# An opening rebuilt around the first batch, with low halves of the weights on GpSimd

## The chip, the cores and the metric

The kernel runs on one core of a Trainium2 chip. A core has a matrix engine (TensorE, PE in the profile), a vector engine (VectorE, DVE), an activation engine (ScalarE, ACT), a general engine (GpSimd, POOL) and a queue engine (SyncE, SP) that issues most transfers. Each engine works through its own instructions in the order in which the program gives them, and waits on semaphores for what the others produce. The metric is the time of one execution in microseconds, taken as the median of several runs.

## What is computed

```python
def _attn_ref(q, k, v, phi):          # 8 batches, 8 heads, 576 rows, 64 wide; phi has 32 columns
    a = phi - np.max(phi, axis=2, keepdims=True)
    a = np.exp(a)
    a = a / (np.sum(a, axis=2, keepdims=True) + 1e-09)
    k_m = np.einsum('bhsm,bhsd->bhmd', a, k)
    v_m = np.einsum('bhsm,bhsd->bhmd', a, v)
    scores = (1.0 / np.sqrt(64)) * np.matmul(q, k_m.transpose(0, 1, 3, 2))
    scores = scores - np.max(scores, axis=-1, keepdims=True)
    attn = np.exp(scores)
    attn = attn / (np.sum(attn, axis=-1, keepdims=True) + 1e-09)
    return np.matmul(attn, v_m)

def _moe_ref(x, w_in, w_out):         # x: 4608 x 512, w_in: 512 x 2048, w_out: 2048 x 512
    h = x @ w_in
    g = h - np.tanh(h)
    return g @ w_out
```

The attention of all batches, laid out as 4608 rows, is the x of the second function. The weights come as 64-bit floats; everything else is 32-bit.

## The kernel before

The 4608 rows are cut into 18 **units** of 256 rows, the 2048 hidden columns into four **quarters** (fb 0 to 3). For each pair of unit and quarter there are a product H (`mm1`: attention weights times a per-batch matrix P, 24 matmuls, or 48 narrower ones where a unit spans two batches), an activation in two steps a and b (`g1`, `g2`: a vector operation each, between ScalarE squares), a third step c (`g3`: the low half of the result, a subtraction), and a product M (`mm2`: 24 matmuls with a quarter of w_out). Every operand is split into two 16-bit halves, so a product takes three matmuls.

Batches have 576 rows: batch 0 serves units 0, 1 and a quarter of 2; batch 1 serves the rest of 2, unit 3 and half of 4. For each batch the attention is made in steps: the maximum over phi's rows (X, XP), the exponential (Y, or XR and YT), pooling of K and V (V, `pool_half`, line 189), its normalisation (N), a turn of the result (U, UV), the scores in two halves of 288 rows (S), and the softmax of those halves. In START it is A and B for batches 0 to 2: line 255 a reduction, line 256 a subtraction, line 257 the exponential, lines 294 to 298 the sum, its reciprocal, the product and a transpose, all on VectorE but the exponential; BH and BL split the result into halves (lines 472, 478). P and PL (`att_p`, `att_pl`) multiply the batch's V matrix with a quarter of w_in.

The weights are loaded as 32 raw blocks of 512 KB (i0 to i15 of w_in, o0 to o15 of w_out). Step T (`conv`) turns two blocks into 32-bit floats with six VectorE instructions (lines 336, 340, 344) and their high halves with two on ScalarE (line 356). Step L (`low_dve`, line 371) makes the low halves with two more on VectorE; one pair of blocks has it done on TensorE (E and K).

The whole opening, up to the first pairs of unit 4, stands in a string START: each word is a step, and the order of the words is the order in which the instructions go into each engine's queue (`in_order` fixes it). `i1:kv3` is a load of block i1 into the buffer kv3. A buffer is reused, so a load waits until the last reader of the buffer is done, and all loads behind it on SP wait too. The first M of a pair of quarters starts an accumulation, the second ends it; for units 0 to 3 the sum over quarters 0 and 1 is written to DRAM and read back in the second half (issued from GpSimd and SP, lines 615 and 646), where a VectorE operation adds it (line 630).

After START a loop over 54 slots (unit 4 quarter 2 to unit 17) takes over, with the attention of batches 3 to 7 placed by PLAN tables relative to the slots; there the softmax's subtraction, product and low half (lines 266, 278, 490) and the third step c (line 570) are on GpSimd. In START no computation is on GpSimd.

PSUM holds two buffers for H ("h"), one for the attention ("pa") and two for M ("o0", "o1").

Of the kernel before, what the change touches and what calls it, by code (L numbers as in the profile page):

```python
# [8 lines left out]
F32 = mybir.dt.float32  # L9
# [9 lines left out]
P = 128  # L19
# [56 lines left out]
N_CHECK = N_F1 + 2 * B + DF // P + DM // P  # L76


class Attention:
# [5 lines left out]
    def load(self, b, d):  # L85
        self.load_phx(b, d)
        self.load_pha(b, d)
        self.load_kv(b, d)
        self.load_q(b, d)
# [5 lines left out]
    def load_pha(self, b, d):  # L95
        nc = self.tc.nc
        d["e"] = self.big.tile([P, 5, 256], F32, tag="e", name=f"e{b}", bufs=1)
        nc.sync.dma_start(d["e"][:, 0:4, :], self.ins["pha"][b])
        nc.sync.dma_start(d["e"][0:64, 4, :], self.ins["pht"][b])

    def load_kv(self, b, d):
        nc, big = self.tc.nc, self.big
        for g in range(4):
            t = big.tile([P, 2, 5, 129], F32, tag=f"kv{g}", name=f"kv{b}{g}", bufs=1)
            nc.sync.dma_start(t[:, :, 0:4, :], self.ins["kva"][b, g])
            nc.sync.dma_start(t[0:64, :, 4, :], self.ins["kvt"][b, g])
            for r in range(2):
                d["kv", g, r] = t[:, r]

    def load_q(self, b, d):  # L110
        nc, big = self.tc.nc, self.big
        for g in range(2):
            x = big.tile([P, 2, S], F32, tag="q", name=f"q{b}{g}")
            nc.sync.dma_start(x, self.ins["qt"][b, g])
            for h in range(2):
                for t in range(2):
                    d["q", 2 * g + h, t] = x[:, h, HS * t : HS * t + HS]

# [959 lines left out]
```

## Time and profile before

| what | value |
|---|---|
| time, median of 3 runs (lowest to highest) | 678.02 us (677.35 to 679.01) |
| span of the profiled execution, first to last instruction | 680.2 us |
| last instruction of START on TensorE (M of unit 3, quarter 3) ends, loop begins | 207.9 us into the span |
| first H, first M | 54.2 us, 68.6 us |
| TensorE busy from 204 us to 640 us | 433.1 of 436 us |

For the profiled execution the page gives the span alone, 680.2 us, and no time of its own; the span is 2.2 us above the median of the three runs. The profile is one page (shares of engines, the span in 40 slices of 17 us, the chain that ended last, the costliest groups of instructions), and further views answer questions: groups of instructions by line and form, the engines' busy time in a stretch, the instructions in order of time, the chain of waits in order of time. A row of a time-ordered view gives start, duration, engine, line, operation, output and inputs with their shapes; "x2" is two merged in one row, and the duration then covers both.

### The profile page before, as it was taken

To read this page: it belongs to the slowest core of one execution; us is meant where nothing else is said; L and a number is where in the kernel's file an instruction comes from. 1 tells how busy PE (TensorE), PEld (TensorE's weight loads), DVE (VectorE), ACT (ScalarE), POOL (GpSimd) and SP (SyncE) were. 2 spreads that over 40 slices of the span, in tenths; PEclk is the share of its full clock that TensorE was granted. 3 is DMA by queue.
4 is the path that set the end of the run, shared out by engine and by line. 5 is a ranking of instruction groups with operands and counts; after the bars stand their busy time and mean duration, and the time that the engine had idled before them with its cause. 6 is when DMAs were issued, how large, how long until landed. Compare 5 with 4: busy or idle time off the path is not lost.

```text
span 680.2 us, 15541 instructions
## 1 busy us (share of the span) xinstructions
PE 645.6 (95%) x6616; PEld 453.7 (67%) x6616; DVE 529.5 (78%) x823; ACT 373.5 (55%) x503; POOL 211.0 (31%) x150
## 2 busy tenths in 40 slices
PE   2588999999999999999999999999999999999995
PEld 2355465664656567777777777777777777887774
DVE  6689999999887677866698768876887586867672
ACT  3246667565544456554565555646555587666541
POOL 0000000000001324452344344534453555455521
PEclk9789999999999999999999999999999999999999
DMA  8956534731341241225331523152415323234101
GB/s 311 359 186 253 197 114 155 219 124 63 133 132 59 83 157 70 68 69 167 97 111 49 177 80 129 38 185 79 137 37 178 98 101 123 79 115 138 60 32 37
DMA packets 38653, 84.99 MB, mean 125 GB/s; under 512 B 4272, under 2 KB 14128, under 8 KB 38576
## 3 DMA queue, kind: packets, MB, share of 16 engines
q1 hardware_dynamic: 37152, 79.59, 35.6%
q0 software_dynamic: 1280, 4.20, 1.6%
q8 instruction: 54, 0.88, 0.5%
q14 instruction: 23, 0.19, 0.1%
q10 hardware_dynamic: 144, 0.13, 0.1%
HBM read 72.37 MB, written 11.53 MB: 123 GB/s over the span
## 4 chain that ended last, share of the span: by engine, by line
PE 70%; DVE 21%; DMA 3%; issue 2%; ACT 2%; SPq 1%; DVEq 0%; ACTq 0%
PE hs L533 18%; PE o L664 12%; PE x L671 12%; PE o L671 9%; PE o L622 9%; PE pkv L189 3%; DVE h L547 3%; DVE h L556 3%; PE h L533 2%; PE pp L500 2%; DVE wt L340 2%; DMA kv<-in_kva_dram 2%; DVE wt L344 2%; DVE f L583 2%; PE psc L237 1%
## 5 line engine op out<-in xcount | busy, mean ns | idle before, releaser
L570 POOL TENSOR_TENSOR g<-h,g 128x1024 f16<-128x1024 f32 x54 | 118.7, 2197 | 246.9 <-ACT g L561 139.9
L533 PEld LDWEIGHTS <-ph 128*128 128x128 f16 x2304 | 176.7, 98 | 21.5 <-issue 6.2
L533 PE MATMUL hs<-ah,ph 128*128 128x256 f16 (+3 forms) x1088 | 145.8, 248 | 0.0
L547 DVE SCALAR_TENSOR_TENSOR h<-hs,u 128x1024 f32<-128x1024 f32 x52 | 63.5, 1221 | 99.1 <-ACT u L539 99.1
L561 ACT ACTIVATE g<-h 128x1024 f16<-128x1024 f32 x72 | 76.1, 1057 | 97.2 <-DVE h L556 97.2
L533 PE MATMUL hs<-al,ph 128*128 128x256 f16 (+3 forms) x544 | 122.1, 247 | 0.0
L552 ACT ACTIVATE u<-u,beta 128x1024 f32<-128x1024 f32 x72 | 82.7, 1148 | 62.6 <-DVE h L547 62.4
L664 PE MATMUL o<-wout_hi,g 128*128 128x512 f16 x416 | 100.6, 379 | 1.6 <-DVE r L731 1.5
L622 PE MATMUL o<-wout_hi,g 128*128 128x512 f16 x320 | 98.6, 379 | 0.7 <-ACT g L561 0.7
L556 DVE SCALAR_TENSOR_TENSOR h<-u,h 128x1024 f32<-128x1024 f32 x72 | 87.7, 1218 | 5.7 <-ACT u L552 5.7
L671 PEld LDWEIGHTS <-f 128*128 128x128 f16 x832 | 81.4, 98 | 9.4
L622 PEld LDWEIGHTS <-g 128*128 128x128 f16 x480 | 45.9, 98 | 58.1 <-issue 3.6
L539 ACT ACTIVATE u<-hs 128x1024 f32<-128x1024 f32 x52 | 53.1, 1022 | 56.2 <-PE hs L533 56.0
L671 PE MATMUL x<-bt,f 128*128 128x256 f16 x624 | 76.6, 273 | 0.0
L671 PEld LDWEIGHTS <-g 128*128 128x128 f16 x624 | 60.9, 98 | 20.8
L664 PEld LDWEIGHTS <-g 128*128 128x128 f16 x416 | 38.6, 98 | 48.4 <-issue 13.4
L583 DVE TENSOR_TENSOR f<-g 128x512 f16<-128x512 f16 x104 | 58.2, 599 | 3.4 <-POOL g L570 3.4
L622 PE MATMUL o<-wout_lo,g 128*128 128x512 f16 x160 | 60.6, 379 | 0.0
L533 PE MATMUL h<-ah,ph 128*128 128x256 f16 (+2 forms) x448 | 55.5, 242 | 0.4 <-DVE h L547 0.4
L533 PE MATMUL h<-al,ph 128*128 128x256 f16 (+2 forms) x224 | 47.9, 242 | 0.0
L646 POOL DMA_DIRECT2D d<-ot x8 | 5.6, 695 | 132.5 <-ACT ot L640 132.5
L512 DVE SCALAR_TENSOR_TENSOR ph<-pp,ph 128x1024 f16<-128x1024 f32 x32 | 38.9, 1217 | 2.6 <-ACT ph L507 2.4
(144 smaller groups left out, 947.3 us busy)
## 6 DMA issues: line engine op xcount, KB each, us to landing
kv<-in_kva_dram SPq DMA_DIRECT2D x40, 258.0 KB, 3.4
raw<-in_w_in_dram SPq DMA_DIRECT2D x16, 512.0 KB, 6.5
raw<-in_w_out_dram SPq DMA_DIRECT2D x16, 512.0 KB, 4.9
chk<-in_w_in_dram SPq DMA_DIRECT2D x16, 512.0 KB, 5.6
chk<-in_w_out_dram SPq DMA_DIRECT2D x16, 512.0 KB, 3.3
out_dram<-r SPq DMA_DIRECT2D x25, 256.0 KB, 2.8
kv<-in_kva_dram SPq DMA_DIRECT2D x12, 516.0 KB, 7.8
q<-in_qt_dram SPq DMA_DIRECT2D x20, 288.0 KB, 3.4
```

The costliest lines, as they stand in the source:

```text
L512: nc.vector.scalar_tensor_tensor(pl, pa, S_P / (S_V * S_W), ph, op0=ALU.mult, op1=ALU.subtract)
L533: nc.tensor.matmul(hp[:, k, tu : tu + w], px[:, g, cs], d[ax][:, g, ta : ta + w], start=(n == 0), stop=(n == 5),)
L539: nc.scalar.activation(uu, hp, AF.Square, scale=1.0 / (S_A * S_P))
L547: nc.vector.scalar_tensor_tensor(h3, hp, C2 * S_G / (S_A * S_P), uu, op0=ALU.mult, op1=ALU.mult)
L552: nc.scalar.activation(uu, uu, AF.Square, bias=c["beta"])
L556: nc.vector.scalar_tensor_tensor(h3, uu, CC, h3, op0=ALU.add, op1=ALU.mult)
L561: nc.scalar.activation(gg[:, 0], h3, AF.Copy)
L570: nc.gpsimd.tensor_tensor(gg[:, 1], h3, gg[:, 0], op=ALU.subtract)
L583: nc.vector.tensor_tensor(o, x, y, op=op)
L622: nc.tensor.matmul(o, gx[:, k, P * tt : P * tt + P], wx[:, 4 * fb + k, :], start=(first and k == 0 and wx is wout_hi and gx is gh), stop=( ...
L664: nc.tensor.matmul(o[th], gg[:, 0, k, P * th : P * th + P], wout_hi[:, 4 * fb + k, :], start=(first and k == 0), stop=False)
L671: nc.tensor.matmul(dst, a(1 - n, kk), b(n, kk), start=(new and kk == 0 and n == 0), stop=(end and kk == 1 and n == 1))
```

## The change

The order of START is rewritten, and some steps change the engine.

- The loads of START begin with the first quarter of w_in and batch 0 alone. phi comes in one transfer per batch instead of two, K and V in two of 1.06 MB and one of 264 KB instead of eight, q in two. Blocks that share a buffer kv2 or kv3 are loaded in pairs, still a transfer each.
- The exponential of batches 0 to 2 is made the one way (X, XP, Y): the way with a turn on TensorE (XR, YT) is gone. `less_top` subtracts the maximum with one operation over four chunks and two over 64 partitions by 128.
- L is on GpSimd for 12 of the 16 pairs: ScalarE first scales the 32-bit block in place, GpSimd subtracts the high half. Lv (4 pairs) stays on VectorE. E, K on TensorE are gone.
- c is on GpSimd for 10 of START's 18 pairs (c), on VectorE for 8 (cv); the two on TensorE (d) are gone.
- The softmax of batches 0 to 2 uses the loop's steps AM, AE, AD, AT, AS: the subtraction, the product and the low half are on GpSimd, five of those 18 on VectorE (AMv, ADv, ASv).
- Units 0 to 3 all do quarters 0 and 1 before any does quarters 2 and 3, with M00, M10, M11, M01, then units 2 and 3; unit 1's first accumulation uses a buffer "h". The partial sums are written by ScalarE's queue (OP, `save_part`), read back by R and finished by O.
- In the loop the pooling of a batch (V) stands one slot later than before for batches 4 to 7, and `less_top` takes the place of the former two GpSimd operations.

```diff
 START = """
-i1:kv3 i0:kv1 FX0 T00 o2:pp5 i2:pp3 L00 o3:pp4 i3:gg KV0 o4:h3 XR0 T09 YT0 o5:uu L09 T01 V0 L01 FX1 Z02 N0 Q0
-U0 i5:h3 T10 Z00 i4:gg L10 UV0 Z06 KV1 XR1 S00 A001 S01 i6:gg Z07 YT1 E02 V1 B001 A012 Z03 N1 B012 U1 UV1
-i7:kv3 K02 BH001 P00 Q1 T03 o0:kv1 BH012 PL00 Z04 Z05 BL001 BL012 Z01 o1:gg L03 S10 H00 P01 T08 PL01 W1 i13:gg
-a00 H10 L08 S11 o7:kv0 i9:kv1 b00 H01 a10 P11 d00 o6:pp5 A102 a01 M00 i8:kv2 T11 b01 i15:kv3 H11 L11 PL11 c01
-b10 i14:pp5 Q2 FA2 M01 B102 d10 BH102 P10 i11:pp4 M10 a11 T07 BL102 b11 o8:kv3 L07 H21 PL10 FX2 H20 c11 T04
-i10:pp5 a20 M11 a21 L04 b20 T05 b21 L05 H31 H30 i12:pp5 c20 M20 c21 a30 W0 T06 o9:kv0 P12 b30 o10:gg L06 PL12
-M21 P02 T12 c30 PL02 o15:pp5 a31 M30 H02 X2 XP2 b31 H12 L12 Y2 o14:h3 c31 o11:gg T15 a02 P03 a12 KV2 M31 L15
-PL03 b02 T13 o13:gg H22 V2 N2 b12 H03 L13 c02 P13 c12 PL13 M02 a03 o12:pp4 U2 a22 T14 b03 H13 L14 c03 b22 a13
-c22 UV2 H23 M03 S20 M12 a23 A201 b13 c13 B201 BH201 P20 M13 PL20 b23 H32 BL201 H33 a32 S21 FQ3 FA3 A212 b32
-B212 W2 M22 c32 P21 PL21 H40 c23 BH212 a33 b33 M23 c33 X3 H41 a40 P23 PL23 BL212 b40 a41 M32 P22 b41 PL22 c41
-M33 c40 KR30
+i1:pp2 i0:gg i2:pp3 FX0 i3:us X0 XP0 Z00 T01 FA0 Y0 KA0 KB0 V00 i4:kv2 Q00 T00 V01 L00 Q01 i6:kv3 Z00 FA1 N0 U0 L01
+o5:pp4 Z00 T02 S00 L02 AM00 S01 UV0 AM01 P00 AE00 AE01 T03 AD00 o4:us o3:pp3 AD01 PL00 AT00 AT01 L03 AS00 o0:gg o2:pp5
+P01 T10 L10 PL01 FX1 KA1 KB1 Q11 H00 AS01 Z00 X1 o1:pp2 a00 XP1 W0 Y1 H10 T09 L09 V10 b00 a10 V11 Q10 H11 N1 o6:gg c00
+o9:pp5 U1 T08 UV1 o8:us L08 b10 H01 o7:pp4 S10 a11 S11 c10 i10:kv3 T11 L11 Q21 T12 M00 AM10 P11 o11:pp5 W1 b11 AM11
+PL11 Q20 M10 c11 AE10 L12 a01 ADv10 P10 M11 AT10 AS10 i8:kv2 OP1 PL10 AE11 b01 o10:qt FA2 c01 H21 T05 L05 ADv11 AT11
+H20 AS11 i14:kv3 M01 FX2 a21 a20 OP0 T04 b20 b21 Lv04 H30 H31 c20 i12:kv2 P02 T13 c21 PL02 L13 a31 a30 M20 X2 KA2 KB2
+P12 b30 PL12 H02 T06 b31 H12 o12:kv2 XP2 M21 c30 Y2 V20 V21 OP2 M30 cv31 Lv06 a02 N2 T07 FA3 Lv07 P03 PL03 M31 OP3 b02
+H03 c02 a12 a03 T14 b12 cv12 U2 UV2 H13 L14 a13 b03 o14:kv3 T15 H22 M02 S20 M12 b13 cv03 P13 Lv15 AM20 a22 M03 PL13 P20
+cv13 W2 R0 O0 H23 R1 PL20 AE20 S21 FQ3 a23 M13 b22 cv22 b23 M22 P21 AMv21 O1 cv23 R2 AD20 PL21 AT20 X3 H33 AE21 H32 a33
+ASv20 M23 a32 b32 b33 O2 ADv21 H40 H41 cv33 c32 P22 a40 a41 PL22 M32 P23 M33 b40 b41 c40 PL23 AT21 R3 AS21 cv41 KR30 O3
 """
+W_TAG = ["pr" if p in (1, 3, 9, 11) else "ot" for p in range(16)]
...
+        d["e"] = self.big.tile([P, 9, 128], F32, tag="e", name=f"e{b}", bufs=1)
+        self.tc.nc.sync.dma_start(d["e"], self.ins["pha"][b])
...
+    def load_kv(self, b, d, rows=(0, 1)):
+        for r in rows:
+            t = self.big.tile([P, 4, 4, 129], F32, tag=f"kv{r}", name=f"kv{b}{r}", bufs=1)
+            self.tc.nc.sync.dma_start(t, self.ins["kva"][b, r])
+            for h in range(4):
+                d["kv", h, r] = t[:, h]
+            if r == 0:
+                self.load_kt(b, d)
+
+    def load_kt(self, b, d):
+        t = self.big.tile([P, 4, 129], F32, tag="kt", name=f"kt{b}", bufs=1)
+        self.tc.nc.sync.dma_start(t, self.ins["kvt"][b])
+        d["kt"] = t
+
...
+        x = self.big.tile([P, 4, HS], F32, tag=tag, name=f"q{b}{t}", bufs=2 if tag == "q" else 1)
+        self.tc.nc.sync.dma_start(x, self.ins["qt"][b, t])
...
+    def less_top(self, eng, e, m):
+
+        eng.tensor_tensor(
+            e[:, 0:8].rearrange("p (c r) x -> p c (r x)", r=2), e[:, 0:8].rearrange("p (c r) x -> p c (r x)", r=2),
+            m.unsqueeze(1).to_broadcast((P, 4, 256)), op=ALU.subtract,
+        )
+        for r in range(2):
+            rs = slice(64 * r, 64 * r + 64)
+            eng.tensor_tensor(e[rs, 8], e[rs, 8], m[rs, 128 * r : 128 * r + 128], op=ALU.subtract)
+
...
+    def pool_half(self, b, d, r, pa=None, ps=None):
+            pa = self.psum(f"pkv{b}{r}", ps)
+        rs = slice(64 * r, 64 * r + 64)
+                hs = slice(32 * h, 32 * h + 32)
+                x, y = (e[:, 2 * c + r, hs], d["kv", h, r][:, c]) if c < 4 else (e[rs, 8, hs], d["kt"][rs, h])
+                nc.tensor.matmul(pa[hs, r, 0:129], x, y, start=(c == 0), stop=(c == 4))
...
-        nc.gpsimd.tensor_tensor(s3, s3, m.unsqueeze(2).to_broadcast((P, NB, 32)), op=ALU.subtract)
+        (eng or nc.gpsimd).tensor_tensor(s3, s3, m.unsqueeze(2).to_broadcast((P, NB, 32)), op=ALU.subtract)
...
-        nc.gpsimd.tensor_tensor(s3, s3, z.unsqueeze(2).to_broadcast((P, NB, 32)), op=ALU.mult)
+        (eng or nc.gpsimd).tensor_tensor(s3, s3, z.unsqueeze(2).to_broadcast((P, NB, 32)), op=ALU.mult)
...
-        ts = [big.tile([P, 512], U32, tag="ot", name=f"wt{p}{i}") for i in range(2)]
+        ts = [big.tile([P, 512], U32, tag=W_TAG[p], name=f"wt{p}{i}") for i in range(2)]
...
-    def low_pe(p):
-        pw = low_ps.pop(p)
+    def low_pool(p):
+        lo = low_of(p)
         for i in range(2):
-            nc.tensor.matmul(pw[:, i], c["nid16"], his[p][:, i], start=False, stop=True)
-        nc.scalar.activation(low_of(p), pw, AF.Copy)
+            nc.scalar.activation(tfs[p][i], tfs[p][i], AF.Copy, scale=S_W)
+            nc.gpsimd.tensor_tensor(lo[:, i], tfs[p][i], his[p][:, i], op=ALU.subtract)
 
...
+        if first and u == 1:
+            t = ps_h.tile([P, 2, DM], F32, tag="h", name=f"o1h{fb}")
+            acc[u] = [t[:, i] for i in range(2)]
+        elif first:
             acc[u] = [ps_o.tile([P, DM], F32, tag=f"o{i}", name=f"o{u}{fb}{i}") for i in range(2)]
...
+    def load_part(u):
+        acc["r", u] = [big.tile([P, DM], F32, tag="pr", name=f"pr{u}{i}") for i in range(2)]
+        for r, p in zip(acc["r", u], parts[u]):
+            nc.sync.dma_start(r, p)
+    def save_part(u):
+        sc = 1.0 / (S_G * S_W)
+        parts[u] = []
+        for tt in range(2):
+            ot = big.tile([P, DM], F32, tag="pr", name=f"ot{u}{tt}")
+            nc.scalar.activation(ot, acc[u][tt], AF.Copy, scale=sc)
+            parts[u].append(dram.tile([P, DM], F32, tag=f"d{u}{tt}", name=f"d{u}{tt}"))
+            nc.scalar.dma_start(parts[u][tt], ot)
+    def save(u):
+        sc = 1.0 / (S_G * S_W)
+        for tt in range(2):
+            o, t0 = acc[u][tt], u * UT + P * tt
+            if u in parts:
+                ot = acc["r", u][tt]
+                nc.vector.scalar_tensor_tensor(ot, o, sc, ot, op0=ALU.mult, op1=ALU.add)
+            else:
+                ot = big.tile([P, DM], F32, tag="pr", name=f"ot{u}{tt}")
+                nc.scalar.activation(ot, o, AF.Copy, scale=sc)
+            nc.sync.dma_start(out[t0 : t0 + P, :], ot)
 
...
-        (-11, "FQ{0} FA{0}"), (-10, "; X{0} KR{0}0"), (-9, "| XP{0} YM{0}"), (-8, "; YE{0} | V{0}0 KR{0}1 N{0}0"), (-7, "| V{0}1 N{0}1 QT{0}0"),
+        (-11, "FQ{0} FA{0}"), (-10, "; X{0} KR{0}0"), (-9, "| XP{0} YM{0}"), (-8, "; YE{0}"), (-7, "V{0}0 KR{0}1 N{0}0 | V{0}1 N{0}1 QT{0}0"),
```

Functions that the new START doesn't call (`conv_p`, `to_size`, `att_pl_p`, `g1_p`, `g2_p`) are added as well and left out here.

More of the change, by code (lines that the diff above doesn't have):

```diff
@@ L88, in load @@
         self.load_kv(b, d)
-        self.load_q(b, d)
+        for t in range(2):
+            self.load_q(b, d, t, "q")
     def load_phx(self, b, d, tag="sc"):
@@ L609, in mm2 @@
         gh, gl = gg[:, 0], gg[:, 1]
-        if first:
+        if first and u == 1:
+            t = ps_h.tile([P, 2, DM], F32, tag="h", name=f"o1h{fb}")
+            acc[u] = [t[:, i] for i in range(2)]
+        elif first:
             acc[u] = [ps_o.tile([P, DM], F32, tag=f"o{i}", name=f"o{u}{fb}{i}") for i in range(2)]
-            if u in parts:
-                acc["r"] = [big.tile([P, DM], F32, tag="pr", name=f"pr{u}{i}") for i in range(2)]
-                for r, p in zip(acc["r"], parts[u]):
-                    nc.sync.dma_start(r, p)
-        both, low = ((wout_hi, gh), (wout_lo, gh)), ((wout_hi, gl),)
-        order = [(0, both), (0, low), (1, both), (1, low)] if last else [(0, both), (1, both), (0, low), (1, low)]
+        both, less = ((wout_hi, gh), (wout_lo, gh)), ((wout_hi, gl),)
+        order = [(0, both), (0, less), (1, both), (1, less)] if last else [(0, both), (1, both), (0, less), (1, less)]
         for tt, part in order:
@@ L1040, in tile_kernel @@
             wide_path(inner, tc, c, ins, out)
[L1043 removed]
+_INS = ["qt", "kva", "kvt", "pha", "phx", "w_in", "w_out"]
 def kernel(**inputs):
```

284 lines of the change are left out of this document (112 added, 172 removed).

## The prediction

> **What bounds the kernel now.** I read the page first, then the engines' busy time by stretch, then the chain of waits in order of time, then single instructions in order of time, and last the groups by line.
>
> ```profile
> span 680.2 us, 15541 instructions
> ```
>
> ```profile
> 0.00:17.00 17.00, 4.26 (x20) 3.78 (x20) 11.14 (x22) 6.04 (x8) 0.95 (x10) 1.00 0.90 311
> 17.00:34.00 17.00, 10.12 (x116) 5.11 (x116) 11.26 (x23) 4.05 (x10) 0.00 (x0) 0.76 1.05 359
> 34.00:51.00 17.00, 15.12 (x167) 8.71 (x168) 14.67 (x31) 7.25 (x13) 0.00 (x0) 0.84 0.57 186
> ...
> 204.00:640.00 436.00, 433.06 (x4672) 322.81 (x4671) 325.73 (x509) 252.22 (x343) 192.68 (x122) 1.00 0.33 105
> ```
>
> ```profile
> 68.58:207.89 139.31, 138.47 (x1234) 80.07 (x1233) 130.49 (x173) 83.36 (x105) 8.79 (x14) 1.00 0.41 139
> ```
>
> The columns are the stretch, its length, busy time (and count) of PE, PEld, DVE, ACT, POOL, the granted clock, the DMA share and GB/s. From 204 to 640 us TensorE is busy 433 of 436 us: the loop is bound by TensorE, and nothing in it gets faster unless TensorE gets less work. What can move is START. The loop's first instruction, and START's first H and M:
>
> ```profile
> 54.16 0.28 PE L533 MATMUL h<-ah,ph 128*128 128x256 f16 x1
> ...
> 68.58 0.38 PE L622 MATMUL o<-wout_hi,g 128*128 128x512 f16 x1
> ...
> 207.89 0.22 PE L533 MATMUL h<-ah,ph 128*128 128x128 f16 x1
> ```
>
> So START ends at 207.9. From the first M at 68.6 TensorE is busy 138.5 of 139.3 us: dense already, beside a VectorE that is busy 130.5. The time before the first M is therefore what can be shortened, and the work behind it. Before the first M there are few products; TensorE waits for VectorE (conversions and softmax), and VectorE at first for data:
>
> ```profile
> 12.20 9.07 DMA kv<-in_kva_dram
> 21.27 0.04 issue
> 21.31 4.99 PE pkv L189 x74
> ...
> 167.22 0.77 PE pp L500 x24
> 167.99 5.35 PE o L622 x24
> 173.35 5.24 PE h L533 x48
> ```
>
> The last K and V of batch 0 land at 21.3. The lower rows give the products' prices: M 5.3, P 0.75, H 2.62 (the row holds two).
>
> **TensorE's work behind the first M.** By the old word order: 16 M = 84.8, 15 H = 39.3, 9 P = 6.8, and V2, U2, XP2, S20, S21 and d10 together some 7.6 (estimates from their rows' neighbours): 138.5, against 139.3 measured, so the count holds. By the new order all of H00, H10, H11 and H01 stand ahead of the first M: 14 H remain, d10 (2.2) is gone, and one P more is left (10). That is -2.6 - 2.2 + 0.75 = -4.1: **135.2 us from the first M to the end of START**, if TensorE stays dense.
>
> **When the first M starts.** Its last input is the w_out half L08, behind T08 on VectorE. First the data. Ahead of the second half of batch 0's K and V now lie i1, i0, i2, i3 (2.10 MB), phi twice (1.18), K and V (2.38): 5.66 MB. The first slice moves 17 us x 311 GB/s = 5.29 MB, the rest at 359: 18.0 us, and with 2.7 us for half the pooling (4.99 us for 74 of 80 matmuls, halved and rounded up) N0 can start at **20.7**. Then VectorE's queue, in word order:
>
> ```profile
> 150.47 0.77 DVE L336 TENSOR_SCALAR wt<-raw 128x512 uint32<-128x512 uint32 x2
> 151.14 1.30 DVE L340 SCALAR_TENSOR_TENSOR wt<-raw,wt 128x512 uint32<-128x512 uint32 x2
> 152.34 1.30 DVE L344 SCALAR_TENSOR_TENSOR wt<-raw,wt 128x512 uint32<-128x512 uint32 x2
> 153.54 1.23 DVE L556 SCALAR_TENSOR_TENSOR h<-u,h 128x1024 f32<-128x1024 f32 x1
> 154.68 1.30 DVE L371 SCALAR_TENSOR_TENSOR wout_lo<-wt,wout_hi 128x512 f16<-128x512 f32 x2
> 155.90 1.23 DVE L566 TENSOR_TENSOR g<-h,g 128x1024 f16<-128x1024 f32 x1
> ```
>
> From start to start T costs 3.07, b 1.14, L on VectorE 1.22; a, PL and cv have the size of b. AT costs 0.78, S (as many elements) 0.84, AM 0.75, AD (a reduction and two operations on 18 numbers) 1.2:
>
> ```profile
> L298 DVE STREAM_TRANSPOSE af<-sc 128x576 f32<-128x576 f32 x4 | 3.1, 778 | 0.2
> ...
> L255 DVE TENSOR_REDUCE sm<-sc 128x18 f32<-128x576 f32 x4 | 2.9, 736 | 0.1
> ```
>
> From N0 to T08 stand five T (15.35), two S, two AM, two AD, two AT (7.1), two PL, a00, b00, a10 (5.7), X1, Y1 (3.3, by their elements), N0, N1 and UV0 (1.9, small operations, estimated): 33.4 us. Without any hindrance T08 ends at 54.1. But GpSimd now works beside it: five L, c00, and AM, AD, AS twice:
>
> ```profile
> L385 POOL TENSOR_TENSOR fy<-chk 128x512 f32<-128x512 f32 x32 | 33.6, 1065 | 0.0
> L490 POOL TENSOR_TENSOR al<-af,ah 128x576 f16<-128x576 f32 x10 | 13.0, 1305 | 8.0 <-ACT ah L489 7.8
> ...
> L266 POOL TENSOR_TENSOR sc<-sc,sm 128x576 f32<-128x576 f32 x10 | 11.6, 1160 | 0.0
> ```
>
> An L is two operations of the first row's size (2.13), c is 2.13 (219.10 below), the softmax steps 1.16 to 1.31: 10.7 + 2.1 + 7.4 = 20.2 us in this stretch. How much of it VectorE pays is the unknown of this case. Four rows of the loop show that it pays at times:
>
> ```profile
> 219.10 2.13 POOL L570 TENSOR_TENSOR g<-h,g 128x1024 f16<-128x1024 f32 x1 [7.94 <-ACT g L561]
> 226.49 3.09 POOL L570 TENSOR_TENSOR g<-h,g 128x1024 f16<-128x1024 f32 x1 [5.26 <-ACT g L561]
> ```
>
> ```profile
> 226.37 1.22 DVE L595 TENSOR_TENSOR bt<-wout_lo,bt 128x2048 f16<-128x2048 f16 x1
> ```
>
> ```profile
> L583 DVE TENSOR_TENSOR f<-g 128x512 f16<-128x512 f16 x104 | 58.2, 599 | 3.4 <-POOL g L570 3.4
> L512 DVE SCALAR_TENSOR_TENSOR ph<-pp,ph 128x1024 f16<-128x1024 f32 x21 | 25.5, 1215 | 0.5 <-ACT ph L507 0.3
> L583 DVE TENSOR_TENSOR f<-g,f 128x512 f16<-128x512 f16 x52 | 23.1, 444 | 1.8
> L583 DVE TENSOR_TENSOR f<-f,g 128x512 f16<-128x512 f16 x52 | 21.6, 415 | 0.0
> ```
>
> The GpSimd operation that met a VectorE operation with two inputs in SBUF took 0.96 us longer than alone, nearly what was left of that operation. The other way round, L583 takes 599 ns on average where its sister forms, of the same size, take 0.42 to 0.44: 104 x 0.17 = 18 us of waiting beside 193 us of GpSimd, a share of 0.1. In START about half of the time belongs to operations of that kind (16 T, 18 b, 8 cv, 4 Lv: 84 of 163 us of VectorE's work), in the loop a third (b and the forms of L583, some 170 of 472). So I take a **share of 0.2** of GpSimd's time as VectorE's wait; the ends are 0 (every meeting falls on operations with one SBUF input, as a, PL and the reductions) and 1. With 0.2 T08 ends at 33.4 + 20.7 + 4.0 = 58.1. L08 adds ScalarE's last high half and first scaling (some 0.6 each, half of L561's elements below) and two GpSimd operations (2.13), 3.5 us with hand-overs: **first M at 61.6**, 7.0 earlier than before.
>
> The Trainium skill, in "SBUF — State Buffer", section "Who interferes with whom", says that a VectorE instruction with two SBUF inputs and a GpSimd instruction that reads SBUF exclude each other for a whole instruction. The row at 226.49 agrees; that it holds for the conversions' operations (L340, L344) no row here shows, since they never met GpSimd. By that rule the share would lie nearer the half than 0.2, and the change would lose; it is the first rival.
>
> **Can the middle stay dense?**
>
> ```profile
> L561 ACT ACTIVATE g<-h 128x1024 f16<-128x1024 f32 x72 | 76.1, 1057 | 97.2 <-DVE h L556 97.2
> ```
>
> The tight place is M20, which needs b20 and c20. VectorE from T08 to b20: four T (12.3), ten a, b, PL (11.4), two ADv with their product (3.9), two AM, S, AT and a UV (5.0): 32.6 us; GpSimd beside it 19.8 us, a fifth is 4.0. So b20 ends at 94.7, c20 at 97.9 (1.06 for the high half, 2.13). TensorE gets there at 61.6 + four M, three P, four H (34.0) = 95.6: 2.3 late. H21 needs AS10: VectorE reaches AT10 at 78.7, and with 2.0 for ah and al 80.7, against 79.0 on TensorE, which the same lateness covers. Behind M21 VectorE has less to do than TensorE (some 71 against 82 us). For uneven hand-overs between four full queues I add 2 us (estimate; 0 at best, and the old order lost 0.8 in 139). ScalarE takes on 12 x 1.2 us of scaling, the four OP and their eight DMA issues, 125 us of work in 200: it has room, but its queue is in order, and OP1 waits there for M11 with AE11 and b01's high half behind it; at 79 to 82 us neither is due earlier.
>
> **Other edits.** Partial sums leave GpSimd's queue for ScalarE's: eight issues, hidden as above; without cover some 0.5 each, as a load on SP (estimate). The clock of the first slices (0.76, 0.84) can fall again with fewer warming matmuls (4 words Z for 8); H00 to H01 have 20 us for 10.5 us of work, so half the clock would still be covered. FX1 is queued on SP behind AT01 (its buffer), with K, V, q and o1 behind it. o1 is the last block that T08 needs, at 16.2 MB: at 359 GB/s it lands at 47.4, and T08 starts at 55: 7.6 us of cover. The loop's V one slot later, its larger transfers and the split GpSimd operation lie beside a TensorE that is busy 99%; I take 0, ends -2 and +3 (its idle time, and a slot's wait in one of four batches).
>
> **The sum.** START ends at 61.6 + 135.2 + 2.3 + 2.0 = 201.1, against 207.9: 6.8 us less. The span becomes 673.4; the medians shown are 2.2 below the span, so 678.0 - 6.8 = **671.2 us**, 1.0% faster.
>
> **Rivals.**
> 1. *GpSimd and VectorE exclude each other fully in START.* For it: 226.49; T is six operations of the kind in a row. Against it: the loop's share of 0.1. With s for the share the end of START is 191.1 + 40 s + 2: it decides from s = 0.37. At 0.5: 213.1, 5.2 us later, **683 us**, slower; at 1 it would be 233, 703 us.
> 2. *Nothing is won ahead of the first M, because the loads set T08.* The third slice moved only 186 GB/s. If the transfers behind FX1 ran at that rate, 11.4 MB by 34 us and 4.8 MB more would be 60 us, T08 5 later: 676 us. Then the larger transfers don't do what they are for. Near no change. ScalarE's or the hand-overs' losing the same 5 us gives the same.
> 3. *VectorE is really freed.* Share near 0 and no lateness: first M at 57.6, end 193, **663 us**. For it: by the prices above VectorE's work in START falls from 185 to 163 us (15 L become 4, -13; 16 c become 8, -9).
>
> **How the numbers follow.** About 0.3% (2 us) is what a measurement of this kernel can tell from no change. Forecast (665 to 676) 0.50; rival 3 and better 0.11; rival 2 and others that end within 0.3% 0.12; rival 1 0.22; worse than 690 by share or by stalls in the loop 0.05. Faster 0.61, same 0.12, slower 0.27. For 8 in 10 the range takes half of rival 3 and the milder half of rival 1: 660 to 685. The likeliest sign's own range is 660 to 676.
>
> **What would show it.** The first H near 41 (54.2 before); the first M near 62; the loop's first H near 201; T, b and Lv rows of START near their old means plus a fifth of GpSimd's busy time (60 us there). Long T rows, with L340 or L344 means well over 0.7 us, show rival 1; a VectorE wait for o0 or o1 shows rival 2; TensorE less than 95% busy after the first M shows my density wrong. The loop's span should stay 472 us; if it doesn't, the PLAN edit was mispriced.

## The result, and the profile after

| | before | after |
|---|---|---|
| time, median (lowest to highest) | 678.50 us (677.35 to 679.01) | 687.84 us (687.42 to 688.35) |
| first H, first M, loop's first H | 54.2, 68.6, 207.9 us | 42.3, 68.1, 214.2 us |

The change makes the kernel **1.4% slower**: ratio 1.0138, 95% interval 1.012 to 1.0156, 9.3 us. The forecast was 671.2 us, with a range of 660 to 685.

The page's first line after, and its engine line:

```profile
span 686.3 us, 15313 instructions
...
PE 636.2 (93%) x6546; PEld 445.1 (65%) x6546; DVE 523.9 (76%) x794; ACT 379.0 (55%) x513; POOL 278.2 (41%) x186
```

The busy time by stretch (length; PE, PEld, DVE, ACT, POOL; granted clock, DMA share, GB/s), and the three landmarks in order of time:

```profile
0.00:17.00 17.00, 3.00 (x10) 1.21 (x14) 8.02 (x16) 3.68 (x4) 0.99 (x11) 1.00 0.90 344
17.00:34.00 17.00, 11.23 (x152) 5.42 (x153) 12.82 (x25) 8.22 (x15) 9.41 (x8) 0.95 0.93 371
34.00:51.00 17.00, 8.99 (x60) 4.75 (x60) 16.83 (x22) 8.38 (x13) 9.86 (x8) 0.65 0.57 223
214.00:640.00 426.00, 423.26 (x4610) 316.58 (x4609) 320.00 (x502) 244.17 (x330) 191.04 (x123) 1.00 0.33 107
68.08:214.16 146.08, 138.16 (x1233) 78.16 (x1227) 126.03 (x159) 85.64 (x111) 47.88 (x27) 0.98 0.39 131
```

```profile
42.32 0.39 PE L527 MATMUL h<-ah,ph 128*128 128x256 f16 x1
...
68.08 0.61 PE L615 MATMUL o<-wout_hi,g 128*128 128x512 f16 x1
...
214.16 0.22 PE L527 MATMUL h<-ah,ph 128*128 128x128 f16 x1
```

Three things are to be seen. The loads are better: 344 and 371 GB/s in the first two slices (311 and 359 before; 325 and 360 in a second profile of the kernel before), and the first H comes 12 us earlier. The first M, which was to come 7 us earlier, comes 0.5 us earlier, and VectorE is busy 16.83 of 17 us ahead of it. Behind it TensorE is idle 7.9 of 146.1 us (0.8 of 139.3 before), at a clock of 0.98. The loop takes 686.3 - 214.2 = 472.1 us, as before (472.3; 470.9 in the second profile): nearly all of the loss lies in START.

What fills VectorE shows in its rows in order of time, and in GpSimd's of the same moments:

```profile
58.32 3.07 DVE L338 TENSOR_SCALAR wt<-raw 128x512 uint32<-128x512 uint32 x2
...
82.18 1.70 DVE L271 TENSOR_SCALAR sz<-sz 128x18 f32<-128x18 f32 x1
...
91.35 3.22 DVE L346 SCALAR_TENSOR_TENSOR wt<-raws,wt 128x512 uint32<-128x512 uint32 x2
...
105.14 1.28 DVE L396 SCALAR_TENSOR_TENSOR win_lo<-wt,win_hi 128x512 f16<-128x512 f32 x2
106.34 0.76 DVE L338 TENSOR_SCALAR wt<-raw 128x512 uint32<-128x512 uint32 x2
107.02 1.28 DVE L342 SCALAR_TENSOR_TENSOR wt<-raw,wt 128x512 uint32<-128x512 uint32 x2
108.22 1.28 DVE L346 SCALAR_TENSOR_TENSOR wt<-raw,wt 128x512 uint32<-128x512 uint32 x2
109.43 1.22 DVE L499 SCALAR_TENSOR_TENSOR ph<-pp,ph 128x1024 f16<-128x1024 f32 x1
111.53 1.23 DVE L541 SCALAR_TENSOR_TENSOR h<-h,u 128x1024 f32<-128x1024 f32 x1 [0.89 <-POOL g L572]
```

```profile
56.55 2.28 POOL L404 TENSOR_TENSOR wout_lo<-wt,wout_hi 128x512 f16<-128x512 f32 x2 [6.10 <-ACT wt L403]
58.79 2.31 POOL L572 TENSOR_TENSOR g<-h,g 128x1024 f16<-128x1024 f32 x1
...
81.72 2.13 POOL L572 TENSOR_TENSOR g<-h,g 128x1024 f16<-128x1024 f32 x1
...
91.36 2.67 POOL L572 TENSOR_TENSOR g<-h,g 128x1024 f16<-128x1024 f32 x1 [2.89 <-issue]
...
105.30 8.28 POOL L572 TENSOR_TENSOR g<-h,g 128x1024 f16<-128x1024 f32 x2 [5.38 <-PE h L527]
```

An operation on 18 numbers a partition (L271 at 82.18) takes 1.70 us and ends at 83.88, just behind a GpSimd subtraction that began at 81.72 and ends at 83.85. T08's first step waits in the same way for L09 and c00 (3.07 us, to 61.39; GpSimd is done at 61.10). The other way round, the third step c of two pairs, c20 and c21, takes 8.28 us in place of 4.26: c20 begins at 105.30, while VectorE goes from one such operation to the next until 109.43; there L499 begins, which has one input in PSUM, and 2.1 us later c20 is done and lets L541 go. TensorE waits for that c (1.12 us ahead of the rest of M20, at 111.56).

TensorE's longest single wait behind the first M is not for GpSimd's result but for the exponential of batch 2, ahead of V20:

```profile
128.15 1.95 PE L189 MATMUL pkv<-kv,e 128*32 128x129 f32 x32 [2.96 <-ACT e L173]
```

It too begins with a meeting. VectorE's first step of T06 takes 2.69 us in place of 0.75, beside c30 on GpSimd (118.92 to 121.15):

```profile
118.75 2.69 DVE L338 TENSOR_SCALAR wt<-raws 128x512 uint32<-128x512 uint32 x2
```

The steps behind it come as much later, among them b31 and the subtraction that the exponential needs (L154 and L160, done at 126.6); the exponential starts at 126.94. Of the 7.9 us of idle time 3.0 are this wait, 3.6 waits for c and al, and 0.8 one for a low half that VectorE makes.

### The profile page after: what moved, and what is told of

It reads as the page before. It is cut to its first block, busy times and chain, and to the rows that moved or that the text cites. A ratio compares the mean times of both kernels' runs of the same rounds, so it can differ in the third digit from the quotient of the medians.

```text
span 686.3 us, 15313 instructions
## 1 busy us (share of the span) xinstructions
PE 636.2 (93%) x6546; PEld 445.1 (65%) x6546; DVE 523.9 (76%) x794; ACT 379.0 (55%) x513; POOL 278.2 (41%) x186
## 4 chain that ended last, share of the span: by engine, by line
PE 69%; DVE 8%; ACT 2%; issue 1%; DMA 1%; POOL 0%; ACTq 0%; SPq 0%; DVEq 0%
PE hs L527 18%; PE o L662 12%; PE x L669 12%; PE o L669 9%; PE o L615 8%; PE h L527 3%; PE pkv L189 3%; PE pp L487 2%; DVE f L585 2%; DVE h L557 2%; DVE h L541 1%; PE psc L232 1%; ACT u L533 1%; DMA kv<-in_kva_dram 1%; PE o1h L615 1%
## 5 line engine op out<-in xcount | busy, mean ns | idle before, releaser
L572 POOL TENSOR_TENSOR g<-h,g 128x1024 f16<-128x1024 f32 x64 | 144.9, 2265 | 304.4 <-ACT g L567 189.6
L541 DVE SCALAR_TENSOR_TENSOR h<-hs,u 128x1024 f32<-128x1024 f32 x52 | 63.5, 1222 | 97.0 <-ACT u L533 97.0
L553 ACT ACTIVATE u<-u,beta 128x1024 f32<-128x1024 f32 x72 | 82.7, 1148 | 61.6 <-DVE h L541 61.6
L662 PE MATMUL o<-wout_hi,g 128*128 128x512 f16 x416 | 100.6, 380 | 1.6 <-DVE r L729 1.6
L557 DVE SCALAR_TENSOR_TENSOR h<-u,h 128x1024 f32<-128x1024 f32 x72 | 89.0, 1239 | 4.5 <-ACT u L553 4.5
L615 PE MATMUL o<-wout_hi,g 128*128 128x512 f16 x256 | 79.3, 381 | 1.1 <-POOL g L572 1.1
L615 PE MATMUL o<-wout_lo,g 128*128 128x512 f16 x128 | 49.0, 383 | 0.8 <-DVE wout_lo L396 0.8
L499 DVE SCALAR_TENSOR_TENSOR ph<-pp,ph 128x1024 f16<-128x1024 f32 x32 | 38.9, 1214 | 3.7 <-ACT ph L494 3.4
L494 ACT ACTIVATE ph<-pp 128x1024 f16<-128x1024 f32 x32 | 32.6, 1017 | 11.8 <-PE pp L487 11.8
```

The lines of the kernel that those rows point to most:

```text
L499: nc.vector.scalar_tensor_tensor(pl, pa, S_P / (S_V * S_W), ph, op0=ALU.mult, op1=ALU.subtract)
L541: nc.vector.scalar_tensor_tensor(h3, hp, C2 * S_G / (S_A * S_P), uu, op0=ALU.mult, op1=ALU.mult)
L553: nc.scalar.activation(uu, uu, AF.Square, bias=c["beta"])
L557: nc.vector.scalar_tensor_tensor(h3, uu, CC, h3, op0=ALU.add, op1=ALU.mult)
L572: eng.tensor_tensor(gg[:, 1], h3, gg[:, 0], op=ALU.subtract)
L615: nc.tensor.matmul(o, gx[:, k, P * tt : P * tt + P], wx[:, 4 * fb + k, :], start=(first and k == 0 and wx is wout_hi and gx is gh), stop=( ...
```

## The experiments

Each kernel is the changed one with the edit shown, unless it says otherwise.

**The kernel before, once more.**

> The kernel before, unchanged, for a second profile. Its first profile has a span of 680.2 us beside a median of 678.5, the changed kernel 686.3 beside 687.8. If the first profile was an ordinary execution, the span is 679 to 681 again and START ends at 207 to 209; if it was a long one, the span is 676 to 678 and START ends near 204, and the 3 us that the two spans don't show of the 9.3 us between the medians lie in START too.

One execution: 678.57 us, span 676.8, first M at 66.64, the loop's first H at 205.93, the loop 470.9 us. The execution whose profile the forecast was worked from (680.2, 207.9) was a longer one than its median, by 2.0 us ahead of the loop and 1.4 in it.

**Most of GpSimd's reads taken away, its time and its waits kept.** Its operations of START read a part of their input and then write constants over the rest: L reads 8 of 512 columns, AM and AD 32 of 576, c a quarter, AS half. The low halves, the third steps and the softmax values that GpSimd makes in START are therefore not computed. Operations that read still take 27.6 of the 80.7 us that GpSimd works in START. The short form writes the constants once.

```diff
+class Blank:
...
+    def tensor_tensor(self, o, x, y, op):
+        k = 8 if len(o.shape) == 2 else 1
+        self.nc.gpsimd.tensor_tensor(o[:, 0:k], x[:, 0:k], y[:, 0:k], op=op)
+        for _ in range(2):
+            self.nc.gpsimd.memset(o[:, k:], 0.03125)
...
-        nc.gpsimd.tensor_tensor(lo[:, i], tfs[p][i], his[p][:, i], op=ALU.subtract)
+        start_eng[0].tensor_tensor(lo[:, i], tfs[p][i], his[p][:, i], op=ALU.subtract)
```

The words c, AM, AD and AS get the same engine in START.

> The changed kernel; in START each GpSimd operation reads only its first few columns and then fills the rest of its output twice with a constant, so it waits for the same inputs and keeps GpSimd busy about as long, but reads next to nothing in SBUF (low halves and attention weights are left out of the result). Exclusion theory: VectorE's waits (about 18 us by the long rows of T, b and the small operations) go, T rows return to 3.07 us each, START ends at 197 to 203 instead of 214, 671 to 677 us. Slow-link theory (GpSimd's own two microseconds per step in the chain): START still ends at 211 to 215. Loads, ScalarE or clock as the cause: 213 to 215.

> As the run before, but each output is filled once, so GpSimd's operations are about half as long. Exclusion theory: within 2 us of the run before, since what matters is gone already. Slow-link theory: START ends some 5 us or more ahead of the run before. Loads, ScalarE or clock: no change.

The long form takes 675.27 us (674.61 to 676.10), ratio to before 0.994 (0.9919 to 0.9961): 12.6 us less than the changed kernel, with GpSimd as busy (279.4 us on the page against 278.2). The short form takes 667.32 (one execution). The long form's stretch from the first M to the loop, and its landmarks:

```profile
63.17:202.92 139.75, 135.53 (x1234) 76.92 (x1227) 122.72 (x161) 85.66 (x112) 48.68 (x79) 1.00 0.40 138
```

```profile
63.17 0.39 PE L627 MATMUL o<-wout_hi,g 128*128 128x512 f16 x1
...
202.92 0.22 PE L539 MATMUL h<-ah,ph 128*128 128x128 f16 x1
```

So with the same order, the same loads and a GpSimd that is as long at work, the opening ends at 202.9, where the forecast had 201.1. What GpSimd reads makes most of the loss.

How long it works is not free either. The short form was expected within 2 us of the long one if the reads were all that counts; it is 8 us faster, with 50.9 us of GpSimd's work in START for 80.7. VectorE's first steps of T are still long in the long form and shorter here (700 and 553 ns on average over START there, 494 and 526 here, 16 operations each: 3.7 us), and GpSimd's results come earlier; the two were not taken apart.

**Nothing of START on GpSimd.** L, c, AM, AD and AS all on VectorE, in the same order of words.

> The changed kernel with everything that START gave to GpSimd back on VectorE (L, c and the softmax steps), in the same word order. VectorE's work in START rises from 163 to about 198 us, its waits for GpSimd (18 us or more) go, ScalarE loses 15 us of scaling. Exclusion theory: most of what moving the work was to bring is given back, so START ends at 214 to 224, at most 10 us later. If VectorE was really relieved by the 35 us, as the forecast had it for four fifths, START ends 25 us or more later, 713 us and more.

698.63 us, ratio 1.0285 (1.0253 to 1.0317), 10.8 us above the changed kernel. The loop's first H is at 226.44, 12.3 us later: a little beyond the 10 that the expectation allowed, and half of the 25 and more of a VectorE really relieved. GpSimd thus does help; it helps by less than its share of the work. This run gives the prices of VectorE's operations when nothing is beside them, here by line and form (count, busy us, mean ns, idle before), and then the same groups of the changed kernel and of the long blanked form (there 12 lines lower):

```profile
L557 DVE SCALAR_TENSOR_TENSOR h<-u,h 128x1024 f32<-128x1024 f32 x18 | 21.6, 1217 | 1.3 <-ACT u L553 1.3
L572 DVE TENSOR_TENSOR g<-h,g 128x1024 f16<-128x1024 f32 x17 | 20.6, 1219 | 8.5 <-ACT g L567 8.4
L346 DVE SCALAR_TENSOR_TENSOR wt<-raws,wt 128x512 uint32<-128x512 uint32 x16 | 10.3, 687 | 0.0
L338 DVE TENSOR_SCALAR wt<-raws 128x512 uint32<-128x512 uint32 x16 | 6.0, 421 | 0.0
L338 DVE TENSOR_SCALAR wt<-raw 128x512 uint32<-128x512 uint32 x14 | 5.3, 422 | 0.1
L271 DVE TENSOR_SCALAR sz<-sz 128x18 f32<-128x18 f32 x6 | 1.1, 177 | 0.2
```

```profile
L557 DVE SCALAR_TENSOR_TENSOR h<-u,h 128x1024 f32<-128x1024 f32 x18 | 23.2, 1301 | 1.3 <-ACT u L553 1.3
L499 DVE SCALAR_TENSOR_TENSOR ph<-pp,ph 128x1024 f16<-128x1024 f32 x12 | 14.5, 1211 | 3.2 <-ACT ph L494 3.1
L346 DVE SCALAR_TENSOR_TENSOR wt<-raws,wt 128x512 uint32<-128x512 uint32 x16 | 12.2, 802 | 0.0
L572 DVE TENSOR_TENSOR g<-h,g 128x1024 f16<-128x1024 f32 x8 | 10.8, 1355 | 2.3 <-ACT g L567 2.3
L338 DVE TENSOR_SCALAR wt<-raws 128x512 uint32<-128x512 uint32 x16 | 10.3, 683 | 0.0
L338 DVE TENSOR_SCALAR wt<-raw 128x512 uint32<-128x512 uint32 x14 | 9.7, 734 | 0.1
L271 DVE TENSOR_SCALAR sz<-sz 128x18 f32<-128x18 f32 x6 | 3.2, 541 | 0.2
```

```profile
L358 DVE SCALAR_TENSOR_TENSOR wt<-raws,wt 128x512 uint32<-128x512 uint32 x16 | 10.3, 686 | 0.0
L350 DVE TENSOR_SCALAR wt<-raws 128x512 uint32<-128x512 uint32 x16 | 10.5, 700 | 0.0
L350 DVE TENSOR_SCALAR wt<-raw 128x512 uint32<-128x512 uint32 x14 | 7.4, 572 | 0.1
```

Read down the means. Two-input operations are lengthened in the changed kernel (L346 687 to 802, L557 1217 to 1301, L572 1219 to 1355) and are back near their price in the blanked form (L358 686; T's other two-input groups 683 to 714, b 1212, c 1220). L499, with one of its inputs in PSUM, is not lengthened (1211; 1219 alone), nor are the reductions (L260 744 in both) and the transposes (L278 766 in both). The fast tensor_scalar, with one input, is lengthened most (L338 421 to 683 and 734, L271 177 to 541), and it stays long beside a GpSimd that mostly writes (L350 700 and 572; one pair of them took 2.30 us at 64.19, where GpSimd wrote constants until 66.2).

**Is it the kind of the operation?** T's first step, in the long blanked form, made an operation with two SBUF inputs (the mask now comes from one column of SBUF, broadcast).

```diff
-            nc.vector.tensor_scalar(
-                t, r[:, :, 1], 3, 0x3FFFFFFF, op0=ALU.logical_shift_left, op1=ALU.bitwise_and
+            nc.vector.scalar_tensor_tensor(
+                t, r[:, :, 1], 3, mask.to_broadcast((P, 512)), op0=ALU.logical_shift_left, op1=ALU.bitwise_and
```

> The blanked run (GpSimd's operations of the opening read a few columns and then write constants twice) had T's second and third steps back at 0.68 to 0.71 us, but the first step, a tensor_scalar with one SBUF input (0.42 alone), still at 0.57 to 0.70 on average and up to 2.30 for two, beside GpSimd operations that only write. Here the first step of every T is a scalar_tensor_tensor whose second input is the mask, broadcast from one column of SBUF: the same result, two SBUF inputs. If an operation with two SBUF inputs is held only by a GpSimd operation that reads, and the fast tensor_scalar by any, the first step is now 0.68 to 0.72 in all rows: 30 x 0.27 = 8 us more work, some 8 us less waiting, time 672 to 679 us. If the first step is held because it comes first behind a pause (place, not kind), its rows stay at up to 2 us for two and the time rises by the 8 us: 681 to 685.

677.63 us, 2.4 above the long blanked form. The first step, by line and form:

```profile
L353 DVE SCALAR_TENSOR_TENSOR wt<-raws,mask 128x512 uint32<-128x512 uint32 x16 | 11.3, 744 | 0.0
L353 DVE SCALAR_TENSOR_TENSOR wt<-raw,mask 128x512 uint32<-128x512 uint32 x14 | 9.2, 700 | 0.1
```

Its waiting falls from 16 x 0.28 + 14 x 0.15 = 6.6 us to 16 x 0.06 + 14 x 0.01 = 1.1, for 30 x 0.265 = 8.0 us more work: net 2.5, and the loop's first H moves by 2.2 (205.11). It is the kind of the operation, not its place. The Trainium skill, "SBUF — State Buffer", section "Who interferes with whom", says both things: a VectorE instruction with two SBUF inputs contends with a GpSimd instruction that reads SBUF, not with one that only writes it; and one in a 2-port mode, which a tensor_scalar can enter, contends with GpSimd, with no such condition. These rows agree with both; that T's first step runs in such a mode no row names, only that it takes 0.42 us where a two-input step of the same size takes 0.69.

**Does VectorE's queue set the first M?** The third step of T (the sign) left out in seven of the sixteen pairs.

```diff
+        if p in (0, 1, 2, 3, 8, 9, 10):
+            return [t.bitcast(F32) for t in ts]
         for r, t in zip(r32, ts):
             nc.vector.scalar_tensor_tensor(t, r[:, :, 1], 0xC0000000, t, op0=ALU.bitwise_and, op1=ALU.bitwise_or)
```

> The third step of the conversion (the sign, 1.20 us from start to start) is left out in T00 to T03 and T08 to T10; five of the seven stand between N0 and the first M. GpSimd, ScalarE, the loads and the order are those of the changed kernel. If VectorE's queue sets the first M, it comes some 6 us earlier (62 in place of 68.1) and the time is 680 to 683. If loads, ScalarE or GpSimd set it, first M stays within 2 us of 68 and the time at 685 to 688.

```profile
62.42 0.39 PE L617 MATMUL o<-wout_hi,g 128*128 128x512 f16 x1
```

683.61 us, just above the 680 to 683 expected. Five steps of 1.2 us ahead of the first M bring it 5.7 us earlier, and 3.7 of these are left at the loop (210.50). Time of VectorE ahead of the first M is paid nearly in full at the first M, and by two thirds at the loop.

**Do the larger transfers count?** K and V in four transfers each.

```diff
-            self.tc.nc.sync.dma_start(t, self.ins["kva"][b, r])
+            for h in range(4):
+                self.tc.nc.sync.dma_start(t[:, h], self.ins["kva"][b, r, :, h])
```

> The changed kernel with K and V of batches 0 to 2 loaded in four transfers each (rows of 2,064 bytes and not 8,256), as small as before, in the same order and into the same tiles. If the larger transfers are what brings N0 from some 25 to 22 us, N0 moves back by 1 to 3 us and the time by as much: 689 to 691. If N0 is early by the order alone (batch 0 ahead of all else), N0 stays at 21 to 22.5 and the time at 687 to 689.

688.41 us, the same; N0 at 22.22 in place of 21.96. The early data come from the order, not from the size of K's and V's transfers.

**Which of GpSimd's work is in the wrong place?** All L (then all c) of START back on VectorE: `L` becomes `Lv`, `c` becomes `cv`, in place.

> All twelve low halves of GpSimd in the opening go back to VectorE. VectorE gets 12 x 1.22 = 14.6 us more, GpSimd 12 x 2.13 = 25.6 us less. With a share of 0.4 VectorE gets 10 us of waits back and is 4 us worse, less what the shorter chain to a low half is worth (up to 2 us): 688 to 692 us. With a share of 0.6 and more it is no worse: 684 to 687. With the share of 0.2 of the forecast it is 9 us worse: 695 to 699.

> All c of the opening that run on GpSimd go back to VectorE (1.14 us each there, 2.13 on GpSimd). Ten c: VectorE +11 us, GpSimd -21 us. Share 0.4: VectorE 3 us worse, 689 to 692; but each c is finished a microsecond or more earlier and no GpSimd operation is kept out for 2 to 4 us (105.30: 8.28 us for two), which is worth up to the 5 us of TensorE's idle time that c and al cause: then 684 to 687. Share 0.2: 694 to 697.

695.24 us with L on VectorE, 686.08 with c. L is better on GpSimd by 7 us. That is at the edge of the branch that the expectation gave to a share of 0.2 (695 to 699), not in that of 0.4 (688 to 692): by its own sum, 14.6 us more work less 25.6 us times the share, 7.4 us of loss are a share of 0.28 for L, or 0.20 if the shorter chain is worth the 2 us that it allows for. c, whose subtraction is kept out longest, comes out 1.8 us better on VectorE, at the bound of what can be told (ratio to before 1.0105, 1.0075 to 1.0135, beside 1.012 to 1.0156 for the changed kernel).

**L on TensorE, as one pair had it before.** The seven low halves ahead of the first M (`L` becomes `Lp`); the second run also has V20 V21 behind M30.

```diff
+    def low_pe(p):
+        pw = ps_h.tile([P, 2, 512], F32, tag="h", name=f"pw{p}")
+        for i in range(2):
+            nc.tensor.matmul(pw[:, i], c["idw"], tfs[p][i], start=True, stop=False)
+            nc.tensor.matmul(pw[:, i], c["nid16"], his[p][:, i], start=False, stop=True)
+        nc.scalar.activation(low_of(p), pw, AF.Copy)
```

> The seven low halves ahead of the first M (L00 to L03, L10, L09, L08) are made as in the kernel before: two products on TensorE and an eviction by ScalarE; their 14 GpSimd operations and 14 scalings go. TensorE has over 25 us of idle time ahead of the first M in the changed kernel, and the new products are 7 x 2.6 = 18 us. If VectorE pays some 0.4 of GpSimd's time, 0.4 x 15 us = 6 us come back: first M at 61 to 64 in place of 68.1, time 680 to 683 us. If GpSimd beside VectorE costs nothing in this stretch (what is late is the chain of data and ScalarE), first M stays at 67 to 69 and the time at 686 to 689. If TensorE's order is what counts, the products delay P and H and it is over 690.

> As the run with seven low halves on TensorE, and V20 V21 stand behind M30, not ahead of it, so that the exp of batch 2 (Y2) has an M to hide behind: the idle 2.96 us of TensorE ahead of V20 should go, so 2 to 3 us less than that run if TensorE is what counts there; no change if VectorE is late by as much just behind.

697.36 and 704.30 us. In the first, what was expected if VectorE gets its time back did not come, and the last branch did: TensorE's order counts, and the first M comes at 79.15. Neither branch of the second came. In the first of the two TensorE stands, in its order, in front of conversions:

```profile
38.65 1.19 PE L403 MATMUL pw<-wt,idw 128*128 128x512 f32 x1 [3.56 <-DVE wt L346]
47.94 0.70 PE L403 MATMUL pw<-wt,idw 128*128 128x512 f32 x1 [3.62 <-DVE wt L346]
```

TensorE had idle time, but behind the waiting product stood P and H, whose results VectorE needs. Moving V20 lost 6.9 us more.

**Attempts at a better order.** e8 puts c and L08 on VectorE and L02, L10, L09 on TensorE where it idles; e11 puts c, AM00, AM01 and L08 on VectorE, S11 behind M00 and the exp of batch 2 earlier; e14, e12 and e13 are parts of e11 (e12 with S11 and M10 placed anew).

> An attempt by the rows of the changed kernel: all c of the opening on VectorE (as in the run with c there, 686.1), L08 on VectorE, and L02, L10, L09 on TensorE at three places where it idles (30 to 39, 47 to 49 and 62 to 65 us), so that GpSimd keeps nine low halves and the softmax steps. If TensorE's order was what made the run with seven low halves there slow, these three cost nothing, VectorE gets 1 to 3 us back ahead of the first M (65 in place of 67.3) and the time is 681 to 684. If TensorE waits for a conversion at any of the three places, it is over 688.

> GpSimd's work is taken off it only where the rows of the changed kernel show it beside a two-input or tensor_scalar operation of VectorE or at the head of TensorE's wait: all c on VectorE, AM00 and AM01 too (they held T03 for 2 us and cost 1.5), L08 on VectorE; S11 stands behind M00, and XP2 Y2 ahead of b31 and M21, so that TensorE needn't wait for exp (2.3 to 3.0 us ahead of V20). If the loss is made at these meetings, first M comes at 65 to 66 and the time is 680 to 684 us, 2 to 6 below the run with c alone (686.1). If VectorE is simply full up to 120 us and each placement only shifts the waits, 685 to 689.

> As e5_c_vector (all c on VectorE, 686.1), and AM00, AM01 and L08 on VectorE too; the order of the words is that of the changed kernel. If the meetings are what is lost, 2 us of T03's waits go for 1.5 us of work and M00 has its low half 2 us earlier, hidden by S11: 685 to 686. If VectorE is simply full, the 2.8 us of added work show: 687 to 689.

> As e14_take_off, with S11 behind M00, its transpose ahead of T12 on VectorE, and M10 ahead of P11. M00 starts at 65 to 66 (e11: 65.12), and P11 needn't wait for 5.7 us. If the start of the first M sets the end, 2 us less than e14: 682 to 685. If VectorE's queue behind M00 sets it, the same as e14, 685 to 689.

> As e5_c_vector, and XP2 Y2 ahead of b31 and M21, so that the exp of batch 2 is done before V20. If TensorE's wait ahead of V20 (2.3 us there) is lost for good, 684 to 685. If VectorE is late by as much just behind, 686 and more.

688.32, 693.32, 688.35, 690.72 and 686.80 us: none is below the run with c alone (686.08), and none came in the branch of its expectation with a gain; e11 and e12 lie above both of their branches. e11 has its first M at 65.12, as expected, and loses it at once:

```profile
76.80 0.63 PE L487 MATMUL pp<-win_hi,vh 64*32 64x512 f16 x8 [5.68 <-DVE sc L241]
```

P11 needs the PSUM tile of S11, and S11's transpose stood behind T11 and T12 on VectorE. With that mended (e12, first M at 66.07) P10 waits 5.03 us, because PL11, which gives the PSUM tile free, stands behind T12, b11 and AM11 on VectorE. VectorE is busy 15.9 to 16.8 of 17 us in each slice from 34 to 102 us of the changed kernel, and an early M or exp only moves the wait. No version here beats the kernel before; only blanked ones do, and they leave work out.

| kernel | us | first M | loop's first H |
|---|---|---|---|
| before, second profile | 678.57 | 66.64 | 205.93 |
| after | 687.84 | 68.08 | 214.16 |
| most of GpSimd's reads blanked, long / short | 675.27 / 667.32 | 63.17 / 59.78 | 202.92 / 195.37 |
| the long form, T's first step with two inputs | 677.63 | 65.00 | 205.11 |
| c on VectorE / L on VectorE / all | 686.08 / 695.24 / 698.63 | 67.29 / 70.76 / 72.39 | 212.32 / 222.47 / 226.44 |
| five third steps fewer ahead of the first M | 683.61 | 62.42 | 210.50 |

## Why the forecast was wrong

The miss is 687.84 - 671.2 = 16.6 us: 13.1 in the end of START (214.2 for 201.1) and 4.0 in the step from span to time, less 0.2 in the loop and 0.3 by which the profiled execution (688.09) lies above its median.

- **The share of GpSimd's time that VectorE pays: the step that failed.** The forecast took 0.2, from the loop's 0.1, and named full exclusion as the first rival, deciding from 0.37. From the means above, with the prices of the run without GpSimd: T's first step 16 x 0.262 + 14 x 0.312 = 8.6 us, its other steps some 3.6, b 18 x 0.084 = 1.5, c 1.1, L271 6 x 0.364 = 2.2, and 1.6 for L140 and AD's product: 18.5 us. GpSimd's own work is 10 c, 24 halves of L and 13 softmax steps, 62.7 us at its prices: a share of 0.30 over START. Up to T08's end it is 0.4: 21.96 + 33.4 = 55.4 without any, 63.8 measured, 8.4 of 20.2 us. Of the 18.5 us 10.7 belong to tensor_scalar operations with one input. The forecast had no reason for these: it counted T whole among the operations with two inputs in SBUF, its first step too, and took operations with one SBUF input for safe. So the sign that it named, L340 or L344 well over 0.7 us (now L342 and L346: 681 to 802 ns), showed only in part; the waits fell on the step ahead of them.
- **What it left out: GpSimd waits too.** GpSimd's START work lasts 76.4 us in place of 62.7:

```profile
L572 POOL TENSOR_TENSOR g<-h,g 128x1024 f16<-128x1024 f32 x10 | 26.2, 2620 | 57.1 <-ACT g L567 45.7 <-issue 6.0 <-PE h L527 5.4
L404 POOL TENSOR_TENSOR wout_lo<-wt,wout_hi 128x512 f16<-128x512 f32 x14 | 20.8, 1507 | 26.6 <-ACT wt L403 26.6
L404 POOL TENSOR_TENSOR win_lo<-wt,win_hi 128x512 f16<-128x512 f32 x10 | 12.1, 1239 | 23.6 <-ACT wt L403 23.6
```

  A c is 2.62 us on average (2.13 alone), an L's half 1.51 and 1.24 (1.06). This delay reaches TensorE through c and al. By the rival's formula (191.1 + 40 s + 2) a share of 0.30 gives 205, of 0.4 gives 209: at 0.30 the kernel would still have gained on 207.9, so the share alone does not explain the loss. Of the 5 to 9 us that are left to 214.2, the later N0 takes 1.3 and the clock 2.6 (both below); the rest, 1 to 5 us, has no term in the forecast. That it is GpSimd's own delay and what follows from it is argued: with most of the reads blanked TensorE's idle time behind the first M falls from 7.9 to 4.2 us, and its wait for the exponential of batch 2 from 3.0 to 0.9, but the waits were not taken away one by one.
- **First M at 61.6, then 139.5 us to the loop** (135.2 of work, 2.3 late, 2 for hand-overs). Measured 68.08 and 146.08; with the reads blanked 63.17 and 139.75. The word count, the prices and the hand-overs held; in the short blanked form, with a first M at 59.78, TensorE runs dense (135.6 us). Of the 6.3 us more than in the blanked run behind the first M 2.6 are TensorE's own (138.16 busy for 135.53, at a clock of 0.98 for 1.00) and 3.7 idle.
- **The clock** was to be covered. Ahead of the first M it was; behind it those 2.6 us fall in two slices, 68 to 85 us (clock 0.95) and 119 to 136 (0.90): the first follows 4.0 us of waiting ahead of the first M, the second holds the 3.0 us wait ahead of V20. That these waits lowered the clock fits, but was not tested. With 138.16 of 146.08 us TensorE is 94.6% busy, just under the 95% that the forecast set for its density.
- **Data.** N0 at 21.96 (forecast 20.7), first H at 42.3 (41). The second rival, that loads set T08, did not happen: T08's first step lies beside GpSimd's L09 and c00, and smaller transfers of K and V change nothing that can be told.
- **The third rival** (VectorE really freed, 663 us) is what the short blanked form comes near, 667 in one execution.
- **The loop** stayed at 472 us (470.1 to 472.5 in the profiles of the table above), and the PLAN edit at nothing, as said.
- **From span to time.** The forecast subtracted 2.2 us from the span, the difference of one long execution to the median of others. A run's own time is 1.8 us above its span (678.57 for 676.8 in the second profile, 688.09 for 686.3 in that after). With 201.1 + 472.3 + 1.8 the forecast would have read 675.2.
- **The rule of the Trainium skill** ("SBUF — State Buffer", "Who interferes with whom") was cited for two-input operations, and the forecast left it as a rival since no row showed a T beside GpSimd. It holds for T's steps, and its second half, on the 2-port modes, was overlooked.

## What to carry to other kernels

Moving work to GpSimd frees VectorE only while VectorE runs operations that don't exclude it: here those with an input in PSUM, reductions and transposes. Before the move, list what VectorE does beside it, count operations with two inputs in SBUF and fast tensor_scalar operations as excluded, and charge both engines. A blanked copy of the work (same time, same waits, few reads) tells in one run whether the reads are what costs; a shorter copy beside it tells what the rest of the other engine's time costs.

## What was not expected of the hardware

- An operation on 18 numbers with one input (L271) costs 177 ns alone and 541 on average beside GpSimd, up to 1.70 us: in that row it ends with GpSimd's operation.
- A GpSimd operation that met a row of such VectorE operations was not let in between them: 8.28 us for two of 2.13.
- Replacing the fast tensor_scalar (0.42 us) by a slower two-input form (0.69) costs 2.4 us in the blanked kernel for 30 operations and not 8, since it no longer waits for a GpSimd that writes.
